# A Fourier filter and a gated feed-forward layer on one core: instructions in the program's own order in place of the scheduler's

## The chip, the cores and the metric

The kernel runs on one core of a Trainium2 chip. The metric is the device time of one execution in microseconds (us); lower is better. A run is told as a median of several executions, most of which agree within 0.3%.

Names used here: TensorE (PE in the profile; PEld is its weight load) multiplies matrices, VectorE (DVE) and ScalarE (ACT) empty PSUM and do elementwise work, GpSimd (POOL) and SyncE (SP) mostly start loads and stores (DMA). The build fixes the order of instructions on each engine.

## The reference, cut to what matters

```python
# x: (8, 3008, 256) float32; filters: 1505 x 256; weights 256 -> 1536 -> 256
def _attn_ref(x, filt_r, filt_i):
    X = np.fft.rfft(x, axis=1)
    Y = X * (filt_r + 1j * filt_i)[None]
    return np.fft.irfft(Y, n=x.shape[1], axis=1).astype(np.float32)

def _moe_ref(x, w_gate, w_val, w_out):          # on (8*3008) rows
    gate = np.maximum(x @ w_gate, 0.0)
    return (gate * (x @ w_val) @ w_out).astype(np.float32)
```

## The kernel before

The transform of length 3008 is split into 94 x 32. Per batch there are three stages of the filter part:

- **A**: 16 fp32 matmuls (`psA`), copied out as `asb`, stored to DRAM (`Abuf`), read back in another layout (`at`);
- **B**: 12 steps. Step g makes `psX` on TensorE, VectorE multiplies it by the two filters (`tt`, `uu`), and one step later TensorE makes `psD` from them; ScalarE copies it out (`dsb`), it is stored (`Dbuf`) and read back (`dC`);
- **C**: small matmuls `psY`, copied out as `yT`, the input of the feed-forward layer. One item is two halves.

The feed-forward layer then works on 8 blocks per batch, each in 12 rounds (`ft`): two value matmuls `psV`, two gate matmuls `psG`, the product on VectorE (`prod`), and three output matmuls `psO` of the block before. The stages A, B and C of batch b+1 are laid into the rounds of batch b. Only batch 0 has nothing to hide behind; the stretch before its first `psV` is called the head below.

```python
# psum: 8 buffers, two for each of the tags "fft", "psv", "psg", "pso".
# psA, psX, psD and psY all take from "fft" (two buffers) after the head.
    def hold_gpsimd(tile_):            # a tiny copy: what follows on GpSimd waits for tile_
        scr = sb.tile([32, 8], BF16, tag="scr", bufs=1)
        nc.gpsimd.tensor_copy(scr, tile_)
# ...
    nc.sync.dma_start(WA, ...)
    load_x(0, nc.sync); load_filters(); load_tables(); load_vg(0)
    # filters: GpSimd queue; tables: ScalarE queue; load_vg(c): a third of the
    # value and gate (up) weights, load_o: W_out, both on the GpSimd queue
    warm(20)                           # 20 matmuls on junk
    for i, f in enumerate(items_a(0)):
        f()
        warm(1)
        if i == 7:
            place_tables(0)            # VectorE copies of the first halves
    load_at(0)
    place_filters(0)

    def after(g, tile_):
        if g == 10:
            hold_gpsimd(tile_[0:32, 5, 0:8])
            load_vg(1)
            load_vg(2)

    for i, f in enumerate(items_b(0, after)):
        if i == 4:
            place_tables(H)            # the second halves
            place_filters(1)
        f()
    load_d(0)
    hold_gpsimd(dCs[0, 0][0:32, 0, 0:8])
    load_o()
    load_x(1, nc.gpsimd)
# ... the feed-forward rounds of batch b:
            for i, f in enumerate(items_a(b + 1)):
                side.setdefault(20 + (3 * i) // 2, []).append(f)
            side.setdefault(45, []).append(lambda b=b: load_at(b + 1))
            for i, f in enumerate(items_b(b + 1)):
                side.setdefault(56 + (7 * i) // 4, []).append(f)
        for ft in range(NFT):
            gv(blk, ft, prods)                         # psV, psG
            if prev is not None:
                o_part(prev[0], ft, prev[1])           # psO
            for f in side.get(z * NFT + ft, ()):
                f()
            if ft in (5, 8) and bi + 1 < len(blocks):
                item_c(*blocks[bi + 1], 0 if ft == 5 else 1)
```

The whole kernel:

In the kernel before, a scheduler in the build decides the order on each engine from this program. So the holds and the place of the warm-ups above are only wishes: the trace shows the loads behind the holds issued long ahead of them.

## Time and profile before

| | us |
|---|---|
| timed, median of 3 (lowest to highest) | 1007.65 (1007.22 to 1008.52) |
| span of the only profile there was before the prediction | 3590.8 |

The profiled execution took 3.56 times as long as the timed ones. From its page: the span, busy times by engine, and the chain of waits that ended last, by engine.

```profile
span 3590.8 us, 18213 instructions
PE 3561.6 (99%) x6756; PEld 1532.6 (43%) x6756; DVE 601.8 (17%) x1062; ACT 581.3 (16%) x1177; POOL 48.5 (1%) x92
...
PE 99%; DMA 1%; ACT 0%; DVE 0%; issue 0%; SPq 0%
```

TensorE is the bound: 99% of the chain. Next, two lines of its timeline (start, length, engine, line, operation, count, and in brackets the idle time before and what ended it).

```profile
11.50 6.83 PE L230 MATMUL psA<-xf,WA 94*96 94x512 f32 x4 [11.50 <-DMA xf<-in_x_dram]
18.01 18.33 PE L369 MATMUL psJ<-junk 128*128 128x512 bf16 x22
```

First, the 22 warm-ups come *after* the first fp32 matmuls although the program has 20 of them before. Second, they take 18.33 us, 0.83 us each for 512 columns. The Trainium skill ("TensorE: Matmul & The Clock Gate", Wait — 56ns, not 53.3ns?) gives N / 2.4 GHz plus about 2.5 ns, so 0.216 us. This profile ran at about a quarter of full rate. From the table of groups (busy us, mean ns of one, then idle time ahead of it):

```profile
L266 DVE TENSOR_TENSOR tt<-psX,Ftr 128x512 bf16<-128x512 f32 x96 | 66.4, 692 | 147.6 <-PE psX L263 139.1
L267 DVE TENSOR_TENSOR uu<-psX,Fti 128x512 bf16<-128x512 f32 x96 | 65.4, 681 | 0.0
```

These are the filter products, 1.37 us per step of B together. Last, the busy times in 5 us stretches (length, busy of PE, PEld, DVE, ACT, POOL with counts, clock, DMA share, GB/s):

```profile
45.00:50.00 5.00, 5.00 (x5) 0.99 (x4) 0.45 (x1) 0.58 (x1) 0.55 (x1) 1.00 0.89 241
50.00:55.00 5.00, 5.00 (x5) 1.23 (x4) 0.90 (x2) 0.00 (x0) 0.00 (x0) 1.00 0.00 0
```

The DMA queues are full until about 50 us and then empty: every load of the head, with weights that are not needed yet, was issued early.

### The profile page before, as it was taken

What the parts mean: (1) busy time and instruction counts of PE and PEld (TensorE: products, weight loads), DVE (VectorE), ACT (ScalarE), POOL (GpSimd) and SP (SyncE); (2) the same over time, 40 slices, a digit from 0 to 9 for tenths busy, and PEclk for the clock granted to TensorE, in tenths of its full rate; (3) what the DMA queues carried; (4) which work ended last, traced back from release to release, by engine and by line L of the source; (5) the groups of instructions that cost most, each with busy time, mean ns of one, the idle gap of its engine ahead of it and who ended that gap; (6) DMA issues with size and microseconds to landing.
All of it is one profiled execution on the core that took longest, in us unless ns stands there. A gap on an engine that the chain in (4) does not pass through costs nothing.

```text
span 3590.8 us, 18213 instructions
## 1 busy us (share of the span) xinstructions
PE 3561.6 (99%) x6756; PEld 1532.6 (43%) x6756; DVE 601.8 (17%) x1062; ACT 581.3 (16%) x1177; POOL 48.5 (1%) x92
## 2 busy tenths in 40 slices
PE   8899999999999999999999999999999999999999
PEld 2333444344443344433444344443444434444444
DVE  2311221112211121111211112110121101211111
ACT  0111111111111111111111111111111111111111
POOL 2000000000000000000000000000000000000000
DMA  6302010110101101001010110101101001010000
GB/s 113 83 21 62 16 33 9 33 49 16 32 9 33 49 17 35 9 30 49 19 33 9 32 51 19 31 7 40 43 19 31 9 18 29 19 31 9 9 9 13
DMA packets 95226, 105.94 MB, mean 30 GB/s; under 512 B 5920, under 2 KB 85984, under 8 KB 92128
## 3 DMA queue, kind: packets, MB, share of 16 engines
q1 hardware_dynamic: 83984, 78.11, 7.5%
q0 software_dynamic: 10176, 25.47, 3.0%
q10 hardware_dynamic: 976, 1.20, 0.2%
q8 instruction: 53, 0.87, 0.1%
q14 instruction: 37, 0.30, 0.0%
HBM read 58.84 MB, written 49.81 MB: 30 GB/s over the span
## 4 chain that ended last, share of the span: by engine, by line
PE 99%; DMA 1%; ACT 0%; DVE 0%; issue 0%; SPq 0%
PE psO L346 26%; PE psV L326 26%; PE psG L326 26%; PE psA L230 12%; PE psX L263 2%; PE psD L277 2%; PE psD L276 2%; PE psY L309 2%; PE psJ L369 1%; DMA xf<-in_x_dram 0%; DMA dC<-Dbuf_74 0%; DMA at<-Abuf_66 0%; DMA WA<-dft_wa 0%; DMA Abuf_66<-asb 0%; DMA Dbuf_74<-dsb 0%; DVE asb L234 0%
## 5 line engine op out<-in xcount | busy, mean ns | idle before, releaser
L346 PE MATMUL psO<-WoT,prod 128*128 128x256 bf16 (+1 forms) x2304 | 1162.4, 692 | 0.0
L326 PE MATMUL psV<-yT,WvT 128*128 128x376 bf16 x1536 | 1144.3, 887 | 0.0
L326 PE MATMUL psG<-yT,WgT 128*128 128x376 bf16 x1536 | 1143.3, 883 | 0.0
L331 DVE SCALAR_TENSOR_TENSOR prod<-psG,vsb 128x376 bf16<-128x376 f32 x768 | 422.1, 550 | 2606.2 <-PE psG L326 2604.2
L346 PEld LDWEIGHTS <-prod 128*128 128x128 bf16 (+1 forms) x2304 | 533.8, 232 | 703.2 <-issue 675.6
L329 ACT CAST vsb<-psV 128x376 bf16<-128x376 f32 x768 | 362.7, 472 | 1630.3 <-PE psV L326 1630.3
L326 PEld LDWEIGHTS <-WgT 128*128 128x128 bf16 x1536 | 341.2, 222 | 584.1 <-issue 584.1
L326 PEld LDWEIGHTS <-WvT 128*128 128x128 bf16 x1536 | 332.1, 221 | 433.8 <-issue 418.2
L230 PE MATMUL psA<-xf,WA 94*96 94x512 f32 x256 | 455.9, 1927 | 11.5 <-DMA xf<-in_x_dram 11.5
L236 ACT CAST asb<-psA 96x512 bf16<-96x512 f32 x120 | 69.8, 582 | 635.5 <-PE psA L230 635.5
L309 PEld LDWEIGHTS <-dC 96*128 96x128 bf16 x512 | 95.2, 216 | 119.6 <-issue 107.9
L277 PE MATMUL psD<-uu,I2u 128*128 128x256 bf16 x192 | 134.3, 699 | 0.0
L276 PE MATMUL psD<-tt,I2t 128*128 128x256 bf16 x192 | 134.0, 698 | 0.0
L230 PEld LDWEIGHTS psA<-xf,WA 94*96 94x96 f32 x256 | 102.6, 413 | 61.5 <-issue 43.0
L309 PE MATMUL psY<-M_83,dC 96*128 96x94 bf16 x512 | 113.4, 425 | 7.1 <-DMA dC<-Dbuf_74 7.1
L279 ACT CAST dsb<-psD 128x512 bf16<-128x512 f32 x96 | 56.3, 586 | 360.5 <-PE psD L277 360.5
L263 PE MATMUL psX<-at,F_84 128*128 128x256 bf16 x192 | 105.1, 692 | 7.3 <-DMA at<-Abuf_66 7.3
L351 ACT COPY osb<-psO 128x512 f32<-128x512 f32 (+1 forms) x128 | 61.3, 479 | 261.3 <-PE psO L346 261.3
L266 DVE TENSOR_TENSOR tt<-psX,Ftr 128x512 bf16<-128x512 f32 x96 | 66.4, 692 | 147.6 <-PE psX L263 139.1
L267 DVE TENSOR_TENSOR uu<-psX,Fti 128x512 bf16<-128x512 f32 x96 | 65.4, 681 | 0.0
L141 POOL DMA_DIRECT2D xf<-in_x_dram x56 | 29.8, 537 | 2390.6 <-PE psA L230 2389.7
L263 PEld LDWEIGHTS <-F_84 128*128 128x128 bf16 x192 | 40.7, 212 | 48.9 <-issue 34.9
(38 smaller groups left out, 236.2 us busy)
## 6 DMA issues: line engine op xcount, KB each, us to landing
xf<-in_x_dram POOLq DMA_DIRECT2D x28, 640.0 KB, 5.5
out_dram<-osb SPq DMA_DIRECT2D x64, 256.0 KB, 2.2
out_dram<-osb SPq DMA_DIRECT2D x64, 120.0 KB
xf<-in_x_dram POOLq DMA_DIRECT2D x28, 112.0 KB, 5.9
xf<-in_x_dram SPq DMA_DIRECT2D x4, 640.0 KB, 10.5
Abuf_66<-asb SPq DMA_DIRECT2D x4, 384.0 KB, 4.4
at<-Abuf_66 SPq DMA_DIRECT2D x4, 384.0 KB, 4.5
Dbuf_74<-dsb SPq DMA_DIRECT2D x4, 384.0 KB, 3.4
```

Of the source, the lines that this page charges most:

```text
L230: nc.tensor.matmul(psA[0:NROW], WA, xf[:, j * 512:(j + 1) * 512], start=True, stop=True)
L236: nc.scalar.copy(dst, psA[0:NROW])
L263: nc.tensor.matmul(psX[:, i], F2[:, g + i, :], at[:, g + i, :], start=True, stop=True)
L266: nc.vector.tensor_tensor(tt, psX, Ftr[:, g:g + 2, :], op=ALU.mult)
L267: nc.vector.tensor_tensor(uu, psX, Fti[:, g:g + 2, :], op=ALU.mult)
L276: nc.tensor.matmul(psD[:, i], I2t[:, g + i, :], tt[:, i], start=True, stop=False)
L277: nc.tensor.matmul(psD[:, i], I2u[:, g + i, :], uu[:, i], start=False, stop=True)
L309: nc.tensor.matmul(psY[:, j * N1:(j + 1) * N1], dCs[b, z // 2][:, (z % 2) * 4 + j, h * 128:(h + 1) * 128], M1, start=True, stop=True)
L326: nc.tensor.matmul(pt[:, :W], w[:, h, ft * 128:(ft + 1) * 128], yt[:, h, :], start=(h == 0), stop=(h == 1))
L329: nc.scalar.copy(vsb, psV[:, :W])
L331: nc.vector.scalar_tensor_tensor(prod, in0=psG[:, :W], scalar=0.0, in1=vsb, op0=ALU.max, op1=ALU.mult)
L346: nc.tensor.matmul(psO[:tw, t % 2], prods[ft][:, t * 128:t * 128 + tw], WoT[:, ft, :], start=(ft == 0), stop=(ft == NFT - 1))
```

## The change

The intent is to have every engine and every load queue follow the program as written. The diff in full:

```diff
+    ctx.enter_context(tc.manual_schedule())
     consts = ctx.enter_context(tc.tile_pool(name="consts", bufs=1))
# ...
     for i, f in enumerate(items_a(0)):
         f()
         warm(1)
-        if i == 7:
-            place_tables(0)
+    place_tables(0)
     load_at(0)
```

## The prediction

> **What bounds the kernel now.** The one profile of the kernel before shows 3590.8 us, while its timed runs take 1007.65 us. A 128x512 warm-up matmul starts every 0.84 us in the timeline. The Trainium skill, "TensorE: Matmul & The Clock Gate" (Seeing it yourself, caveats), reports the clock gate sometimes stuck at a quarter and its records unreliable; this trace agrees with that: its clock record says 1.0, yet 512 columns / 2.4 GHz would be 0.213 us, so TensorE ran at about a quarter. So I use the trace for order, DMA and other engines, and divide TensorE spacings by 3.94.
>
> TensorE busy is 3561.6 us (page, part 1), so about 905 us at full rate: 90% of 1007.65 us. The chain of waits: 99% TensorE. VectorE (601.8 us) and ScalarE (581.3 us) have slack. About 100 us remain; I estimate that most is the head, batch 0, before the first block of the second part: x lands (first matmul at 11.5 us), then 16 fp32 matmuls and 36 warm-ups (estimate 23 us at full rate), a trip through DRAM (write 4.4, read 4.5 us), 12 steps of the filter stage bound by VectorE (0.692+0.681 us each, 17 us), and another trip (3.4 us write, about 3.5 us read).
>
> **What the change does.** It only moves work. I wrote out the program's order by hand and compared it with the trace. From the first block on they differ by one or two neighbours per batch: 0 +- 3 us. In the head:
> - The 20 warm-ups run before x is there, not after its first matmuls: 22 x 0.84 us in the trace, 4.7 us at full rate. Gain up to 4.7 us.
> - The 7 table loads come after all 8 x loads. The load queue's own waits show x loads waiting 3.9 us for table loads[...]. x lands earlier by some us. ScalarE, which issues table loads, now waits for x loads to land (estimate until 18 to 20 us) before its first copy; with two PSUM buffers TensorE stalls at the fifth fp32 matmul. Cost: 3 us.
> - The GpSimd queue's holds now come before the second and third thirds of the up weights, W_out and x of batch 1. In the trace these were issued by 44 us and DMA is saturated (1.0 to 1.36) until 47 us, just where Abuf is written and read. Gain: about 3 to 4 us.
> - VectorE places the second halves of tables and filters inside the filter stage: 6 x 0.355 + 4 x 0.952 = 5.9 us, on its critical path. Before, most of these filled idle VectorE time. Loss: 4 to 6 us.
> Net: about -5 us.
>
> **Predicted: 1002 us, range 989 to 1012.** Faster by over 2%: 0.10; within 2%: 0.86; slower: 0.04.
>
> **What shows it right.** In the timeline, warm-ups precede the first fp32 matmul; ScalarE's first copy waits for an x load; no weight loads lie between the first Abuf write and the end of the at reads; a 6 us gap between tt/uu products in batch 0; the first psV starts 3 to 8 us earlier if TensorE runs at full rate; durations and block order unchanged.
>
> **What makes it wrong.** A load held back too long (W_out is needed 8 us after the first block begins, x of batch 1 some 16 us after) stalls the first blocks. If scheduled order costs stalls in the steady state at full rate, which this slow profile hides, the gain exceeds 2%. If the ScalarE queue stalls longer, the head gets longer.

## The result

| | before | after |
|---|---|---|
| timed, median us (4 runs each) | 1007.78 | 1010.26 |
| lowest to highest | 1007.22 to 1008.52 | 1009.60 to 1011.08 |
| ratio, 95% interval | | 1.0025 (1.0007 to 1.0042) |

A ratio is the mean time of one kernel's fast runs over that of the kernel before in the same rounds, so not quite the ratio of the medians quoted. The measured time lies inside the stated range, but that is luck: a gain of about 5 us was forecast and a loss of 2.5 us came.

The profile after ran at full rate, so the first profile of before cannot stand beside it. The kernel before was run once more for that; it is the first experiment.

> The kernel before, unchanged, to get a profile at full TensorE rate (the first one ran at about a quarter). Theory A (only the head differs, as predicted: the first 100 us): first psV of block 0 between 73 and 80 us against 77.0 us in the changed kernel, about 3 us earlier; steady batches of 118.7 us as in the changed kernel. Theory B (the steady state differs): the first psV comes as late as or later than 77 us and a batch takes about 118.3 us or less.

It took 1009.89 us in its single run (state unknown, but its span of 1008.1 us and clock 0.983 are those of the fast runs). Of the two theories above, B came true: the first `psV` comes at 86.61 us and a batch takes 117.28 us. All lines of "before" from here on are from this second profile. Line numbers after the change are one higher. Busy times, before and then after:

```profile
PE 956.9 (95%) x6756; PEld 658.3 (65%) x6756; DVE 584.7 (58%) x1062; ACT 548.1 (54%) x1177; POOL 49.3 (5%) x92
```

```profile
PE 960.0 (95%) x6756; PEld 659.6 (65%) x6756; DVE 587.4 (58%) x1062; ACT 548.6 (54%) x1177; POOL 48.0 (5%) x92
...
PE 91%; DMA 4%; DVE 3%; ACT 1%; issue 1%; SPq 0%; ACTq 0%
```

The second line of the fence after is its chain of waits. TensorE is 3 us busier after, at the same count. That says nothing yet. The stretches do: the first 100 us and the 200 us that follow, before, then after (columns as above).

```profile
0.00:100.00 100.00, 52.49 (x230) 25.52 (x231) 46.67 (x79) 20.78 (x39) 24.16 (x44) 0.83 0.88 176
100.00:300.00 200.00, 199.86 (x1413) 137.42 (x1412) 119.83 (x219) 117.00 (x252) 8.38 (x16) 1.00 0.38 110
```

```profile
0.00:100.00 100.00, 62.83 (x290) 32.50 (x291) 51.16 (x87) 25.79 (x49) 22.70 (x44) 0.81 0.86 179
100.00:300.00 200.00, 197.50 (x1402) 136.17 (x1401) 119.72 (x217) 116.01 (x251) 8.42 (x16) 1.00 0.38 112
```

Two opposite changes. In the first 100 us TensorE is busy 10.3 us longer after (62.83 against 52.49) and has 290 matmuls behind it in place of 230. In the 200 us that follow it stood idle 0.14 us before and 2.5 us after. The SyncE queue shows the first of these; `x4` are four DMA issues, with the start of the first and the time to the end of the last. Before, then after:

```profile
...
29.47 11.61 SPq L238 DMA_DIRECT2D Abuf<-asb  x4
47.04 7.99 SPq L251 DMA_DIRECT2D at<-Abuf  x4
...
81.56 1.73 SPq L298 DMA_DIRECT2D dC<-Dbuf  x4
```

```profile
...
18.30 15.04 SPq L239 DMA_DIRECT2D Abuf_68<-asb  x4
40.43 2.31 SPq L252 DMA_DIRECT2D at<-Abuf_68  x4
...
72.05 1.73 SPq L299 DMA_DIRECT2D dC<-Dbuf_76  x4
```

| head, us | before | after |
|---|---|---|
| last matmul of A ends (after: a warm-up) | 39.37 | 32.46 |
| first `psX` of B | 58.46 | 43.91 |
| last `psD` of B ends | 75.19 | 66.39 |
| first `psV`, end of the head | 86.61 | 77.00 |
| first `psX` of batch 1 | 154.82 | 146.14 |
| time from one batch's first `psX` to the next | 117.28 | 118.71 |
| last matmul ends | 1004.85 | 1005.90 |

The head is 9.6 us shorter in these two profiles. From the first `psX` of batch 1 to the end the kernel after is 9.7 us slower (859.76 against 850.03). So the expected gain was there, larger than forecast, and it was given back in the part that the prediction had put at 0 +- 3 us. The head is less sure than the batches: both profiled executions were slower than their medians (1009.89 and 1011.08 us), and the traces end 1.05 us apart where the medians differ by 2.5. With seven batches 1.43 us longer each, 10.0 us, the medians leave an estimated 7.5 us for the head.

Where it was given back shows in the timeline. Batch 1 after the change, first at the second step of B:

```profile
146.14 0.38 PE L264 MATMUL psX<-at,F_86 128*128 128x256 bf16 x2
...
147.43 0.68 DVE L268 TENSOR_TENSOR uu<-psX,Fti 128x512 bf16<-128x512 f32 x1
...
148.17 0.39 PE L264 MATMUL psX<-at,F_86 128*128 128x256 bf16 x2 [0.51 <-DVE uu L268]
```

The first `psX` (step 0) was made at 146.14 us, in round 56 of the batch before. One round later the program calls step 1. There are two "fft" buffers: one holds step 0's `psX` until VectorE is done with `uu`, the other was taken by the `psY` of the same round. So TensorE waits 0.51 us for `uu`. The same place before:

```profile
154.82 0.38 PE L263 MATMUL psX<-at,F 128*128 128x256 bf16 x2
...
156.17 0.48 PE L326 MATMUL psV<-yT,WvT 128*128 128x376 bf16 x2
156.49 0.32 PE L326 MATMUL psG<-yT,WgT 128*128 128x376 bf16 x1
...
156.85 0.39 PE L263 MATMUL psX<-at,F 128*128 128x256 bf16 x2
```

The scheduler put `psV` and half of `psG` of the next round ahead of the second `psX`. The 0.51 us were filled with work. The second place, after:

```profile
163.67 0.27 PE L278 MATMUL psD<-uu,I2u 128*128 128x256 bf16 x1
...
163.98 0.59 ACT L280 CAST dsb<-psD 128x512 bf16<-128x512 f32 x1 [0.66 <-PE psD L278]
...
164.61 0.33 PE L310 MATMUL psY<-M_85,dC 96*128 96x94 bf16 x4 [0.67 <-ACT dsb L280]
```

This is round 68, the other one with `ft` 8 and a step of B. The program calls C's second half in it, so `psY` follows `psD` directly and needs a buffer that ScalarE has yet to empty: 0.67 us. The scheduler had put `psY` one round later, between `psO` matmuls:

```profile
171.65 0.27 PE L277 MATMUL psD<-uu,I2u 128*128 128x256 bf16 x1
...
172.40 0.27 PE L346 MATMUL psO<-WoT,prod 128*120 128x256 bf16 x1
...
172.60 0.33 PE L309 MATMUL psY<-M,dC 96*128 96x94 bf16 x4
...
172.76 0.40 PE L346 MATMUL psO<-WoT,prod 128*120 128x256 bf16 x2
```

Who waited for whom on TensorE between 100 and 1000 us, after (us in total, times, longest):

```profile
PE psY L310 <- ACT dsb L280: 4.7, 7, 0.7
PE psX L264 <- DVE uu L268: 3.6, 7, 0.5
```

Seven batches, seven times each, 8.3 us together. The same view of the kernel before is empty. That is most of the 9.7 us. The rest is not in shorter gaps: from the first `psX` of batch 1 to the end TensorE is idle 8.73 us after and 0.42 us before. A stop costs more than the view lists, because the wait is counted from the end that the profile gives to the matmul before, and in an unbroken stream the next one starts ahead of that end: three `psO` of 0.49 us start at 145.81 us, and the `psX` behind them at 146.14. So each stop takes an estimated 0.16 us more, 0.68 and 0.83 us in place of 0.51 and 0.67, which is 10.6 us in seven batches; the batches say 10.0 us, since the kernel before has small stops of its own.

### The profile page after: what moved, and what is told of

Same layout as the page of the kernel before. It is cut to its first block, busy times and chain, and to the rows that moved or that the text cites. A ratio compares the mean times of both kernels' runs of the same rounds, so it can differ in the third digit from the quotient of the medians.

```text
span 1009.2 us, 18208 instructions
## 1 busy us (share of the span) xinstructions
PE 960.0 (95%) x6756; PEld 659.6 (65%) x6756; DVE 587.4 (58%) x1062; ACT 548.6 (54%) x1177; POOL 48.0 (5%) x92
## 4 chain that ended last, share of the span: by engine, by line
PE 91%; DMA 4%; DVE 3%; ACT 1%; issue 1%; SPq 0%; ACTq 0%
PE psO L347 24%; PE psV L327 24%; PE psG L327 24%; PE psA L231 11%; PE psY L310 2%; PE psD L277 2%; PE psD L278 2%; PE psX L264 2%; DMA xf<-in_x_dram 2%; DVE uu L268 1%; DVE tt L267 1%; DMA Abuf_68<-asb 1%; DMA Dbuf_76<-dsb 0%; ACT dsb L280 0%; DVE prod L332 0%
## 5 line engine op out<-in xcount | busy, mean ns | idle before, releaser
L347 PE MATMUL psO<-WoT,prod 128*128 128x256 bf16 (+1 forms) x2304 | 375.0, 273 | 0.0
L327 PE MATMUL psV<-yT,WvT 128*128 128x376 bf16 x1536 | 371.9, 323 | 0.2 <-ACT yT L316 0.2
L327 PE MATMUL psG<-yT,WgT 128*128 128x376 bf16 x1536 | 371.1, 323 | 0.0
L347 PEld LDWEIGHTS <-prod 128*128 128x128 bf16 (+1 forms) x2304 | 246.0, 110 | 90.0
L327 PEld LDWEIGHTS <-WgT 128*128 128x128 bf16 x1536 | 149.8, 98 | 96.2 <-issue 1.6
L327 PEld LDWEIGHTS <-WvT 128*128 128x128 bf16 x1536 | 143.7, 98 | 63.8 <-issue 52.2
L231 PE MATMUL psA<-xf,WA 94*96 94x512 f32 x256 | 131.1, 593 | 1.5 <-DMA xf<-in_x_dram 1.0
L310 PE MATMUL psY<-M_85,dC 96*128 96x94 bf16 x512 | 42.6, 206 | 14.3 <-DMA dC<-Dbuf_76 9.6
L277 PE MATMUL psD<-tt,I2t 128*128 128x256 bf16 x192 | 50.0, 284 | 6.4 <-DVE tt L267 5.9
L278 PE MATMUL psD<-uu,I2u 128*128 128x256 bf16 x192 | 49.6, 283 | 1.5 <-DVE uu L268 1.4
```

The costliest lines, as they stand in the source:

```text
L231: nc.tensor.matmul(psA[0:NROW], WA, xf[:, j * 512:(j + 1) * 512], start=True, stop=True)
L277: nc.tensor.matmul(psD[:, i], I2t[:, g + i, :], tt[:, i], start=True, stop=False)
L278: nc.tensor.matmul(psD[:, i], I2u[:, g + i, :], uu[:, i], start=False, stop=True)
L310: nc.tensor.matmul(psY[:, j * N1:(j + 1) * N1], dCs[b, z // 2][:, (z % 2) * 4 + j, h * 128:(h + 1) * 128], M1, start=True, stop=True)
L327: nc.tensor.matmul(pt[:, :W], w[:, h, ft * 128:(ft + 1) * 128], yt[:, h, :], start=(h == 0), stop=(h == 1))
L347: nc.tensor.matmul(psO[:tw, t % 2], prods[ft][:, t * 128:t * 128 + tw], WoT[:, ft, :], start=(ft == 0), stop=(ft == NFT - 1))
```

## The experiments

All of these kernels gave the reference's result; all profiles but the first of before ran at full rate.

Theory B: the steady state loses 0.67 + 0.51 us per batch because the program's order puts instructions next to each other that share a PSUM buffer. Rival: the longer batches come from DMA or from the order on the other engines. For the head there is theory A: the program's order is better there except for the second halves of tables and filters. "Beside after" below means the difference of the two kernels' distances from the medians of before in their own rounds (after: +2.5 us).

### C's second half one round earlier

```diff
-            if ft in (5, 8) and bi + 1 < len(blocks):
+            if ft in (5, 7) and bi + 1 < len(blocks):
```

> The changed kernel with the second half of the third stage's item at ft 7 in place of ft 8, where it meets a step of the filter stage. Theory B1 (per batch, TensorE loses 0.67 us because psY comes right behind psD in the program's order and takes its PSUM buffer, and 0.51 us at the second step of the filter stage): the 0.67 us gap goes in all 7 batches, a batch takes 118.0 us in place of 118.71, 4 to 5 us less: about 1005.5 us, 0.998 of before. Rival (the longer batches come from something else, such as DMA or the order on ScalarE or VectorE): batches stay at 118.7, about 1010 us.

Measured: 1000.87 us, ratio 0.9928 (0.9915 to 0.9940), 9.8 us less beside after; a batch takes 117.45 us, 1.26 us less. That is about twice what was expected. The waits view between 100 and 1000 us:

```profile
PE psD L277 <- DVE uu L268: 2.1, 7, 0.3
```

The `psY` wait is gone, and so is the `psX` wait: with `psY` moved out of round 56, its buffer is free when step 1 comes. What is left is 0.3 us for `uu` itself. So the place of C's second half was behind both waits, in rounds 56 and 68; the expectation had counted only one of them.

### B's first step one round earlier

```diff
-                side.setdefault(56 + (7 * i) // 4, []).append(f)
+                side.setdefault(56 + (7 * i) // 4 - (i == 0), []).append(f)
```

> The changed kernel with the first step of the filter stage one ft earlier (55 in place of 56), so that its products are done when the second step comes. Theory B1: the 0.51 us gap before the second psX goes in all 7 batches, a batch takes 118.2 us, 3 to 4 us less: about 1006.8 us, 0.999 of before. Rival: batches stay at 118.7 us, about 1010 us.

Measured: 1005.55 us, ratio 0.9969 (0.9956 to 0.9981), 5.2 us less beside after; a batch takes 118.04 us. The waits view:

```profile
PE psY L310 <- ACT dsb L280: 4.7, 7, 0.7
PE psD L277 <- DVE yT L318: 0.3, 1, 0.3
```

The `psX` wait is gone, the `psY` wait stands unchanged at seven times 0.67 us, and a wait of 0.3 us comes once. The `psX` wait can be taken away without the other, and the time follows: 0.68 us per batch, the estimated cost of that stop. Nothing was changed for DMA in these two runs, and the order of work on the other engines only where it follows the two moves. The rival falls.

### The same two moves under the scheduler

> The kernel before (scheduler's order) with the two moves of the steady state that took 9.4 and 4.7 us off the changed kernel when each was made alone. If the scheduler had already moved the colliding instructions apart (its batches take 117.28 us without a gap over 0.3 us): at most 2 us less, 1006 to 1008 us, batches of 117.0 to 117.3 us. Rival (the two moves are simply a better place for the work, whatever the order): 8 to 10 us less, about 999 us.

Measured: 1005.14 us against 1009.03 in its rounds, ratio 0.9964 (0.9950 to 0.9979); a batch takes 116.98 us against 117.28. That is more than the 2 us at most that were expected, and less than half of the rival's 8 to 10. Of the 3.9 us, 2.1 us are the seven batches. The first `psV` came at 83.68 us in place of 86.61; up to the first `psV` the order is the same on every engine, so these 2.9 us are the spread of the head between executions. In program order the two moves together are worth 1.73 us per batch (118.71 to 116.98, in the last version below), under the scheduler 0.3 us: it had already moved the colliding instructions apart.

### Second halves of tables and filters ahead of stage B

```diff
     place_filters(0)
+    place_tables(H)
+    place_filters(1)
# ...
     for i, f in enumerate(items_b(0, after)):
-        if i == 4:
-            place_tables(H)
-            place_filters(1)
         f()
```

VectorE's timeline after the change, in stage B of batch 0:

```profile
49.02 0.68 DVE L268 TENSOR_TENSOR uu<-psX,Fti 128x512 bf16<-128x512 f32 x1
...
51.84 1.94 DVE L196 COPY Ftr<-Ftr 32x3072 bf16<-32x3072 bf16 x2
53.80 1.94 DVE L196 COPY Fti<-Fti 32x3072 bf16<-32x3072 bf16 x2
55.77 0.69 DVE L267 TENSOR_TENSOR tt<-psX,Ftr 128x512 bf16<-128x512 f32 x1
```

Between the `uu` that ends at 49.70 us and the `tt` at 55.77 us VectorE does nothing but such copies, and TensorE stands idle 5.54 us:

```profile
56.52 0.40 PE L277 MATMUL psD<-tt,I2t 128*128 128x256 bf16 x1 [5.54 <-DVE tt L267]
```

> The changed kernel with the second halves of tables and filters placed on VectorE before the filter stage, where VectorE sits idle from 39.6 to 44.5 us. Theory A (that placing, in the middle of the filter stage, costs what the other moves gain): the 5.5 us gap of TensorE at 51 us goes, one of about 1 us comes before the first tt, so 4 to 5 us less than the changed kernel: about 1006 us, 0.998 of before. Theory B (the loss lies in the steady state): VectorE is not what binds the head, no change, about 1010 us, 1.0025 of before.

Measured: 1005.04 us, ratio 0.9968 (0.9955 to 0.9982), 5.8 us less beside after. The first `psV` came at 71.81 us in place of 77.00; batches stayed at 118.71 us. This part of the prediction (a loss of 4 to 6 us) was right. It also shows that there is not one loss only: this one is in the head, the waits of the batches stand beside it.

### The weights early again

```diff
     load_vg(0)
+    load_vg(1)
+    load_vg(2)
+    load_o()
# ... and removed behind the two holds
```

> The changed kernel, but the second and third thirds of the up weights and W_out are issued right behind the first third, as the scheduler had them, not held back; x of batch 1 stays held. Theory A (the holds keep the DMA queues free for the DRAM trip between fp32 matmuls and filter stage, which is why that trip took 11.5 us in place of 19.1): the trip grows by 4 to 8 us, so about 1015 us, 1.007 of before. Rival (the trip is shorter only because the last Abuf write is issued earlier, the holds matter little): trip within 2 us of 11.5, about 1010 us.

Measured: 1012.43 us, ratio 1.0038 (1.0023 to 1.0054), 1.7 us more beside after. The stretch from the last matmul of A to the first `psX` grew from 11.45 to 16.38 us. The DMA issues between 32 and 60 us (KB of each, median us to landing), after, then with weights early:

```profile
at<-Abuf_68 SPq DMA_DIRECT2D x4, 384.0 KB, 4.2
```

```profile
at<-Abuf SPq DMA_DIRECT2D x4, 384.0 KB, 10.3
```

The read of `at` took 10.3 us in place of 4.2 beside the weight loads. The Trainium skill ("DMA: Bandwidth & Descriptors", Queues, rings and completion order) says that each DMA engine takes turns between the queues that have work; this trace agrees that another queue's loads slow the read down. But 2.0 us come back at the end of the head, where no weights are left to load: TensorE waits 7.55 us for `dC` in place of 9.55. The mechanism was as expected, the total 2.7 us at the first `psV` and not 4 to 8.

### Warm-ups late

```diff
-    warm(20)
     for i, f in enumerate(items_a(0)):
         f()
-        warm(1)
+        warm(20 if i == 1 else 1)
```

> The changed kernel with its 20 warm-up matmuls behind the second fp32 matmul in place of ahead of the first, about where the scheduler had them. Theory (their place is worth up to 4.7 us in the head, as predicted): the last fp32 matmul of batch 0 ends 3 to 5 us after 32.5 us and the total is 1013 to 1015 us. Rival (the fp32 stage is bound by the landing of x and by the Abuf writes, so the place matters little): within 1.5 us of 1010.3.

The edit also leaves out one of the 36 warm-ups. Measured: 1011.14 us, ratio 1.0024 (1.0008 to 1.0041): no difference from after. A ended at 36.09 us in place of 32.46, yet the SyncE queue reads

```profile
...
23.74 13.23 SPq L239 DMA_DIRECT2D Abuf<-asb  x4
40.48 2.24 SPq L252 DMA_DIRECT2D at<-Abuf  x4
```

and the `at` loads go out at 40.48 us, as in the kernel after (40.43). They wait for the last store of `Abuf` to land, for 6.9 us in the kernel after and 3.4 us here: it was issued 3.6 us later and landed at the same time. So the matmuls did not set that time. What did was not tested; the other loads in the DMA queues are likely. In this order the prediction's gain of up to 4.7 us is off the critical path: it is worth 0.

### Filter copies among the evictions of stage A

In the kernel before, VectorE stood idle for 6.36 us until 26.90 us, when a filter load landed, and only behind that copy could it empty the next `psA`:

```profile
26.90 0.95 DVE L195 COPY Fti<-Fti 32x3072 bf16<-32x3072 bf16 x1 [6.36 <-DMA Fti<-in_filt_i_dram]
```

This puts that back:

```diff
         warm(1)
+        if i == 2:
+            place_filters(0)
     place_tables(0)
     load_at(0)
-    place_filters(0)
```

> The changed kernel with the first halves of the filters placed on VectorE among the evictions of batch 0's fp32 stage (behind the third item), as the scheduler had done, so that VectorE waits there for a filter load (it landed at 26.9 us in the scheduler's kernel). Theory (this held up the head before: first Abuf write at 29.5 us against 18.3): the first Abuf write goes to 28 to 30 us, the filter stage starts 3 to 6 us later than 43.9 us, total 1013 to 1016 us. Rival (the filter stage's start is bound by DMA traffic ahead of the last Abuf write, as in the run with late warm-ups, where 3.6 us later fp32 matmuls cost nothing): within 1.5 us of 1010.3.

Measured: 1014.68 us, ratio 1.0070 (1.0055 to 1.0085), 4.2 us more beside after. The SyncE queue and VectorE's timeline:

```profile
...
29.78 12.59 SPq L239 DMA_DIRECT2D Abuf<-asb  x4
45.19 2.29 SPq L252 DMA_DIRECT2D at<-Abuf  x4
```

```profile
16.36 0.69 DVE L235 CAST asb<-psA 96x512 bf16<-96x512 f32 x1 [9.47 <-PE psA L231]
...
26.25 0.99 DVE L196 COPY Fti<-Fti 32x3072 bf16<-32x3072 bf16 x1 [3.65 <-DMA Fti<-in_filt_i_dram]
...
29.01 1.28 DVE L235 CAST asb<-psA 96x512 bf16<-96x512 f32 x2
```

The eviction that follows at 29.01 us had been held behind copies that waited for filters, the first store of `Abuf` goes out at 29.78 us in place of 18.30, and the `at` loads 4.8 us later than in the kernel after. The prediction does not have this term: of the copies it says only that those of the second halves filled idle VectorE time. The slow profile did not show the cost: VectorE waited 2.87 us for the same filter load there, but was done with it at 26.96 us, and its next `psA` came only at 43.78.

### Both, and with x of batch 1

The early weights and the filter copies among the evictions, together (1.7 and 4.2 us when each was made alone):

> Both the early weights and the filter copies among the evictions, in the changed kernel. If these two orders are what made the scheduler's head 9.6 us longer: the filter stage starts at 55 to 59 us (58.5 in the scheduler's kernel, 43.9 in the changed one) and the total is 1017 to 1021 us, 1.010 of before (less is lost at the end of the head, where no weights are left to load). If more of it comes from elsewhere (x of batch 1, second filter halves, warm-ups): the filter stage starts before 53 us.

Measured: 1017.76 us, ratio 1.0092 (1.0075 to 1.0109). The first `psX` came at 53.94 us, short of the 55 to 59 expected, so something was still missing. The next run adds x of batch 1 as the scheduler had it: first chunk right behind `W_out`, two at the first hold, one at the second.

> head_as_before, with the loads of batch 1's x also as the scheduler had them: its first chunk right behind W_out, the next two at the first hold, the last at the second. Theory (that chunk is in flight while at is read, and makes the read slow: the at loads took 12.1 us to landing in the scheduler's kernel): the filter stage starts 3 to 5 us later than in head_as_before (53.9 us), at 57 to 59 us, the total is 1019 to 1023 us. Rival (x of batch 1 has no part in it): 53 to 55 us, 1017 to 1018 us.

Measured: 1023.79 us, ratio 1.0144 (1.0127 to 1.0161), slightly more than expected; first `psX` at 57.50 us (before: 58.46), first `psV` at 91.40. Unlike the kernel before this one still has the second halves inside stage B, which cost 5.2 us above; less those, 91.40 becomes an estimated 86.2, against 86.61 before. On that estimate, and with the spread of the head in mind, the head's difference is accounted for by four orders: filter copies among the evictions, weights, x of batch 1, and, in the other direction, the second halves.

### The other half of the diff

Moving `place_tables(0)` alone, under the scheduler, compiles to the same order of instructions on every engine, so it was not run. In program order with the old place:

> The changed kernel with the first halves of the tables placed behind the eighth fp32 matmul, as before: the second part of the diff undone. VectorE waits at most 1 us for a table load there, and the copies (2.2 us) hold back two evictions; the filter stage waits for the at load and not for VectorE. Expected 1010 to 1012 us, so this part of the diff is worth 0 to 1.5 us; a rival that gives it the loss would see 1007 us or less.

Measured: 1009.99 us, ratio 1.0011 (0.9996 to 1.0027), an interval that overlaps the one of after. This part of the diff is worth too little to tell.

### A version that beats both

The two moves of the steady state and the early second halves together, in program order.

> The changed kernel with both moves in the steady state and the second halves of tables and filters placed before the filter stage of batch 0. If the three effects are separate and add: 1010.3 - 5.2 - 8 to 9 = 996 to 998 us, 0.989 of before, batches of 117.3 us as in the kernel before. If the steady state is longer for another reason: 1005 us, as place_early.

Measured: 992.76 us, ratio 0.9845 (0.9832 to 0.9859), batches of 116.98 us, first `psV` at 71.67 us. That is 3 us better than expected, for the most part because the batches came down further than to the 117.3 us of the expectation.

No wait of TensorE is left in the waits view between 100 and 1000 us: from the first `psX` of batch 1 to the end it is never idle, and the same holds for sched_steady_fix with the same batches. So without the collisions the two orders cost the same in the steady state, and what is left between them, 1005.14 against 992.76 us, is the head: first `psV` at 83.68 us against 71.67. This version is 1.5% faster than before and, from the ratios, 1.8% faster than after. The three single gains beside after (9.8, 5.2 and 5.8 us) sum to 20.8 us and 17.9 came. Two of them take away the same wait of `psX`: per batch they give 1.26 and 0.68 us alone and 1.73 us together, 1.5 us less than their sum over seven batches. The rest is within the intervals of the ratios.

One more try, 76 warm-ups laid into the two idle stretches of the head:

```diff
+    warm(40)
     place_tables(0)
# ...
+    warm(36)
     load_d(0)
```

> all_fix with 40 warm-ups in the gap of the first DRAM trip and 36 in that of the second. In all_fix the first ten matmuls of block 0 start every 0.31 us in place of 0.16, at a lower clock. If that lower clock comes from the idle time ahead of it: about 2 to 3 us less, 990 us. If the warm-ups only delay work or the clock falls anyway: 993 us or more.

Measured: 992.16 us, ratio 0.9834 (0.9819 to 0.9849): not to be told from all_fix. The stretches at the end of the head (length, busy times, clock, DMA share, GB/s):

```profile
68.00:70.00 2.00, 0.39 (x2) 0.00 (x0) 0.00 (x0) 0.00 (x0) 0.00 (x0) 1.00 1.01 305
72.00:74.00 2.00, 2.00 (x9) 0.97 (x7) 1.10 (x2) 1.04 (x3) 2.00 (x5) 0.53 1.10 234
76.00:80.00 4.00, 4.00 (x32) 2.50 (x31) 3.22 (x7) 3.05 (x7) 1.06 (x2) 1.00 1.24 266
```

The clock still fell to half, in the middle of dense matmuls at 72 us, after only 1.73 us of idle time ahead of the first `psY`. The same low stretch came, a little later, so nothing was gained. Why it fell was not found. The warm-ups run on a constant tile; neither other data nor a longer row of them, up to the last moment, was tried.

## Why the prediction was wrong, point by point

- **"From the first block on they differ by one or two neighbours per batch: 0 +- 3 us." This is the step that failed.** The two neighbours were found in the trace ahead of time, but their cost was not worked out. They were the scheduler's answer to a shortage of two PSUM buffers. The waits are 1.18 us per batch, the batches 1.43 us longer, and from the first `psX` of batch 1 to the end 9.7 us were lost. The prediction named this risk the wrong way round: it feared that the *scheduled* order had stalls that the slow profile hid. It was the program's order that had them.
- **Head, "about -5 us" net.** It was -9.6 us in the profiles (7.5 us estimated from the medians). The sum was mis-sized in several terms that partly cancel:
  - warm-ups, "up to 4.7 us": 0 (late_warm), off the critical path;
  - "x lands earlier", ScalarE "waits for x loads", "cost: 3 us": did not happen. The table loads kept their place, from 0.7 us on in both profiles, and x took as long to issue. ScalarE's first copy waited for `psA`, at 14.16 us;
  - holds, "3 to 4 us": 2.7 us for the weights alone, and more with x of batch 1 (6.9 us between the first `psV` of head_as_before and head_with_x);
  - second halves, "loss 4 to 6 us": 5.2 us, right;
  - filter copies among evictions: not in the prediction; first `psV` 4.9 us later when put back (81.85 against 77.00).
- **What bounds the kernel** (TensorE, about 905 us of work at full rate): right in kind, but TensorE is busy 957 us in the full-rate profile. The divisor 3.94 was too large: a steady batch takes 441.5 us in the slow profile and 117.28 in the full-rate one, 3.76, which gives an estimated 947 us. What makes up the rest was not looked into; the half-clock stretches of the head (mean clock 0.83 in the first 100 us) are part of it.
- **Signs.** The warm-ups came first, the 6 us gap in stage B came, durations stayed. The first `psV` came 9.6 us earlier, more than the 3 to 8 us given. "No weight loads lie between the first Abuf write and the end of the at reads" was wrong: the first third of the up weights is issued at 31.4 us, behind the filters.
- **"Faster by over 2%: 0.10; within 2%: 0.86."** The outcome lies within 2%, but by luck: a larger gain and a larger loss cancelled.

## What to carry to other kernels

When a program takes over from a scheduler, compare the two orders and cost every place where they differ: ask which buffer the displaced instruction waits for, and multiply by the number of times it comes. Two items that take from the same small pool of PSUM buffers should not be called in the same round; here one number, 8 to 7, was worth 9.8 us of a 1010 us kernel. A change that is neutral in sum can be a gain and a loss; with its losses taken away it ran in 992.8 us, against 1005.1 us for the scheduler's order with the same two moves.

## What the Trainium skill lacked or had wrong

- "TensorE: Matmul & The Clock Gate" (Seeing it yourself) tells of a clock stuck at a quarter for over 50 us and of unreliable records. Here a whole profiled execution ran like that, 3590.8 us against 1007.65 us timed, with a recorded clock of 1.0 throughout.
- The same page (Why this matters for your kernels) says to leave no idle gaps over about 3 us. In all_fix_warm the clock fell to about half (0.53 over 72 to 74 us) during dense matmuls, with only 1.73 us and 0.39 us of idle time in the 12 us ahead of it. That is one profile, and its warm-ups ran on a constant tile.
- No page gives the cost of PSUM reuse between neighbours in an engine's order: here, by the waits view, 0.67 us when `psY` follows `psD` directly and 0.51 us when `psX` follows one round behind, both for a pool of two buffers; the batches grew by an estimated 0.16 us more for each.
- No page says how much a load queue that is full slows a read from another queue: here the 384 KB reads of `at` took 4.2 us alone, 10.3 us beside weight loads, and 12.1 us beside weights and x.
